# Memory rows leave the attention's sum after its column-tiled products, and TensorE's order is searched anew

## The chip, the cores and the metric

The kernel runs on one core of one Trainium2 chip. The metric is the device time of an execution in microseconds (us).

## The reference, cut to what matters

Two layers run one after the other, each an attention with recurrent memory and a gated FFN. The attention goes through 64 segments of 32 rows. Eight memory rows, the first rows of a segment's output, are put ahead of the next segment's rows:

```python
mem = mem0
for s in range(n_seg):                                   # 64 segments
    h = jnp.concatenate([mem, xs], axis=1)               # 8 + 32 rows of 576
    q, k, v = (jnp.einsum('btd,dhe->bhte', h, W) for W in (Wq, Wk, Wv))   # 32 heads of 128
    p = _softmax(jnp.where(mask, q @ k * scale, -1e9))
    o = jnp.einsum('bhte,hed->btd', p @ v, Wo)
    mem = o[:, :M, :].copy()                             # M = 8
    outs.append(o[:, M:, :])
```

So a segment's Q, K and V cannot be complete before the last output product of the segment ahead of it. (The three einsums and the score lines are shortened here.)

## The kernel before

The kernel runs both layers as a pipeline: in most of the 71 steps one segment of each layer is worked on, 2 x 40 columns side by side. TensorE runs its groups of matmuls in an order that is written down as a string of letters. The string was found by a search; a planning model in Python then fills in the other engines' order and the buffers.

The letters that matter: Q = a part of Q and K (32 products of 128x128 weights with 80 columns), q = its tail (rows 512 to 575 of the width 576, row-tiled), S = scores, T = transposes of the probabilities, P = probabilities times V, O = output product of a group of eight heads (32 products), o = its tail (output columns 512 to 575, column-tiled, 8 products), V/v and X/x = values, F/f = FFN up, W = FFN down (8 products), a, b, n, p = transposes for normalisations and residuals.

The sum of the output products is one PSUM bank, YB, with five chunks of columns: 0 to 3 from O, 4 from o.

```python
def wo(self, t, g, ot):                       # O
    ...
            for db in range(4):
                self.mm(yT[:, db, :], self.T.WO[:, GH * g + hl, db * P:(db + 1) * P], OT[:, hl, :], ...)

def wo_tail(self, t, g, ot):                  # o
    ...
            r = R64 * (hl % 2)
            self.mm(yT[r:r + R64, 4, :], self.T.WO[:, GH * g + hl, 4 * P:D], OT[:, hl, :], ..., tile_position=(0, r))
```

At the end of a step ScalarE copies the memory rows of chunks 0 to 3 from YB to HT, the transposed input rows of the next step. I call this "the copy". Chunk 4 comes in two halves that have to be added: ScalarE copies one to YO, VectorE adds the other. The dependencies that the planning model is given:

```python
yo = node("ACT", actc(c80), em.y_odd(t), deps=wots[3:], ...)
if nxt:
    ye.append(node("ACT", actc(4 * m), em.y_mem(t, nxt, 0), deps=wos[3:], prio=t - 0.01, name="Ymem"))
    ye.append(node("DVE", dve(m, m), em.y_mem(t, nxt, 1), deps=[yo] + ye, prio=t - 0.005, name="Ymem"))
ht_mem[t + 1] += ye
yts = [node("ACT", actc(*([128] * nl)), em.yts(t, ls, 0), deps=wos[3:] + ye, ...)]
```

`wos` are the step's O groups, `wots` its o groups. The copy depends on the last O alone, so the model may put it between the o groups. It is only a plan of the order: the semaphores come afterwards, from what the instructions of the program in that order read and write.

## Time and profile before

| | before |
|---|---|
| median time, 3 runs | 2802.13 us (2796.95 to 2804.0) |
| TensorE busy | 2730.5 us, 98% |
| VectorE, ScalarE busy | 72%, 40% |
| TensorE waits, YB products behind the copy | 43 of 70 steps |

TensorE has something in flight nearly always, so its busy share tells little of what could be saved. What does is the spacing of matmul starts: within a group it is steady, and between two groups it is nearly the same for the same pair of letters every time, unless something is waited for. From the records of start times I summed three things: spans from the first to the last start of each group (2279.2 us), usual pauses between groups (475.4 us), and excess over the usual pause (42.0 us, counting excesses above 0.06 us). All pauses together are 504.8 us, 12.6 less than the last two give, as many pauses are a little shorter than the usual one. The records follow the order string, except that 16 of the 60909 products (all in o groups) start up to 0.05 us ahead of the last product of a group of scores. The lines of the profile are shown in the prediction.

### The profile page before, as it was taken

Reading aid. Unit: us, or ns where it says so; the run is one execution under the profiler, and the core shown is the slowest. Engines: PE = TensorE matmul, PEld = TensorE weight load, DVE = VectorE, ACT = ScalarE, POOL = GpSimd, SP = SyncE. Lnnn points to the kernel's source line nnn. Section 1 sums busy time; section 2 is a strip of 40 time slices with the busy share of each in tenths; the row PEclk is TensorE's granted clock in tenths of the full one; section 3 lists DMA queues with packets and bytes.
Section 4 is the critical chain, followed back from the end, with each engine's and each line's share of the span. In section 5 each row is a group of like instructions: output and inputs, shape, how many; then the busy total and the mean of one; then the engine's idle time right before and its main releaser. Section 6 shows DMA issues by size and latency. Waiting matters only on the chain.

```text
span 2798.6 us, 136339 instructions
## 1 busy us (share of the span) xinstructions
PE 2730.5 (98%) x60909; PEld 2252.9 (81%) x60909; DVE 2018.1 (72%) x5501; ACT 1116.7 (40%) x3422; POOL 328.4 (12%) x399
## 2 busy tenths in 40 slices
PE   5999999999999999999999999999999999999998
PEld 4787878888888888888888888888888788888886
DVE  4677777777777677777767777776777777677765
ACT  2434443443434344343434434343443434343332
POOL 1111110110101011010101101010110101010110
PEclk9999999999999999999999999999999999999999
DMA  8072524234251523425152342515234251423568
GB/s 306 17 197 83 162 67 138 65 112 130 62 153 48 152 73 111 132 60 153 49 148 77 111 131 60 150 52 145 81 111 131 60 147 54 142 82 109 143 177 248
DMA packets 483438, 323.80 MB, mean 116 GB/s; under 512 B 26297, under 2 KB 478401, under 8 KB 481185
## 3 DMA queue, kind: packets, MB, share of 16 engines
q1 hardware_dynamic: 479824, 308.15, 37.6%
q8 instruction: 476, 7.80, 1.2%
q0 software_dynamic: 3024, 6.93, 0.8%
q14 instruction: 114, 0.93, 0.1%
HBM read 310.26 MB, written 2.36 MB: 112 GB/s over the span
## 4 chain that ended last, share of the span: by engine, by line
PE 96%; DMA 1%; ACT 1%; issue 1%; DVE 1%; POOL 0%; SPq 0%; DVEq 0%; ACTq 0%; POOLq 0%
PE bank L538 83%; PE YB L538 14%; DMA W<-in_A_Wk_dram 1%; ACT HT L541 0%; DMA W<-in_A_Wq_dram 0%; ACT OT L541 0%; DVE STAT L544 0%; DVE SME L544 0%; DVE PB L544 0%; ACT PTS L541 0%; DVE HTT L544 0%; ACT SME L541 0%; DVE PTS L544 0%; DVE XR L544 0%; DVE XN L544 0%
## 5 line engine op out<-in xcount | busy, mean ns | idle before, releaser
L538 PEld LDWEIGHTS <-W 128*128 128x128 bf16 (+1 forms) x29040 | 1227.2, 98 | 158.8 <-issue 53.6
L538 PE MATMUL bank<-HT,W 128*128 128x80 bf16 (+3 forms) x22720 | 815.5, 198 | 20.4 <-DMA W<-in_A_Wk_dram 11.7
L538 PE MATMUL bank<-XTB,W 128*128 128x256 bf16 (+3 forms) x6320 | 654.6, 262 | 1.4 <-issue 1.3
L895 POOL MEMSET PB<- 128x1024 bf16 x284 | 270.0, 951 | 2119.2 <-PE bank L538 1682.6
L541 ACT ACTIVATE QKT<-bank 128x64 bf16<-128x64 f32 (+1 forms) x1381 | 316.1, 315 | 364.2 <-PE bank L538 335.5
L538 PE MATMUL YB<-OT,WO 128*128 128x80 bf16 (+3 forms) x11360 | 429.4, 199 | 20.6 <-ACT HT L541 13.5
L538 PEld LDWEIGHTS <-WO 128*128 128x128 bf16 (+1 forms) x11400 | 389.0, 101 | 55.8 <-issue 39.3
L538 PE MATMUL bank<-WV,HT 128*32 128x512 bf16 (+1 forms) x6840 | 384.4, 382 | 0.0
L544 DVE CAST QKT<-bank 128x64 bf16<-128x64 f32 (+2 forms) x683 | 186.2, 316 | 238.7 <-PE bank L538 236.7
L541 ACT ACTIVATE HTT<-bank 128x512 bf16<-128x512 f32 (+1 forms) x324 | 177.8, 551 | 392.9 <-PE bank L538 391.5
L538 PE MATMUL bank<-W2C,HTT 128*128 128x288 bf16 x2232 | 320.7, 287 | 0.4 <-DMA W2C<-in_B_w_dram 0.4
L544 DVE TENSOR_REDUCE STAT<-SME 104x8 f32<-104x320 f32 (+1 forms) x568 | 271.8, 479 | 51.3 <-ACT SME L541 47.0
L544 DVE TENSOR_TENSOR PB<-SME,STAT 40x128 bf16<-40x128 f32 (+1 forms) x1004 | 283.5, 321 | 15.5
L538 PEld LDWEIGHTS <-HT 128*32 128x32 bf16 (+1 forms) x6840 | 149.4, 95 | 166.8 <-issue 42.8
L538 PEld LDWEIGHTS <-HTT 128*128 128x128 bf16 x2304 | 206.4, 98 | 59.2 <-issue 6.9
L544 DVE SCALAR_TENSOR_TENSOR XR<-bank,XR 128x288 f32<-128x288 f32 x576 | 239.6, 448 | 11.7 <-PE bank L538 7.2
L544 DVE SCALAR_TENSOR_TENSOR HTT<-HTT,bank 128x512 bf16<-128x512 bf16 (+1 forms) x324 | 201.9, 623 | 55.4 <-ACT HTT L541 53.4
L541 ACT ACTIVATE PTS<-bank 128x320 bf16<-128x320 f32 (+1 forms) x413 | 157.1, 414 | 177.6 <-PE bank L538 120.9
L544 DVE TENSOR_TENSOR HTT<-HTT,bank 128x512 bf16<-128x512 bf16 (+1 forms) x324 | 203.5, 628 | 22.3 <-PE bank L538 0.5
L541 ACT ACTIVATE OT<-bank 128x320 bf16<-128x320 f32 (+1 forms) x379 | 147.0, 412 | 171.1 <-PE bank L538 170.9
L541 ACT ACTIVATE SME<-SME 104x320 f32<-104x320 f32 (+1 forms) x284 | 133.5, 470 | 202.5 <-DVE SME L544 202.3
L544 DVE TENSOR_TENSOR SME<-bank,maskb 104x320 f32<-104x320 f32 (+1 forms) x284 | 133.9, 485 | 104.6 <-PE bank L538 102.8
(64 smaller groups left out, 1671.4 us busy)
## 6 DMA issues: line engine op xcount, KB each, us to landing
W<-in_B_w_dram SPq DMA_DIRECT2D x612, 256.0 KB, 3.8
W2C<-in_B_w_dram SPq DMA_DIRECT2D x306, 288.0 KB, 3.2
W<-in_B_w_dram SPq DMA_DIRECT2D x612, 32.0 KB, 3.4
W<-in_B_w_dram SPq DMA_DIRECT2D x10, 512.0 KB, 8.7
WO<-in_A_Wo_dram SPq DMA_DIRECT2D x4, 1152.0 KB, 18.3
XR<-in_A_x_dram POOLq DMA_DIRECT2D x16, 288.0 KB, 4.6
W<-in_A_Wq_dram SPq DMA_DIRECT2D x4, 1024.0 KB, 8.0
W<-in_A_Wk_dram SPq DMA_DIRECT2D x4, 1024.0 KB, 16.8
```

The source lines that it names most:

```text
L538: self.ch("PE", self.nc.tensor.matmul(out, lhsT=lhsT, rhs=rhs, start=start, stop=stop, skip_group_check=True, **k))
L541: self.ch("ACT", self.nc.scalar.activation(*a, **k))
L544: self.ch("DVE", getattr(self.nc.vector, fn_)(*a, **k))
L895: return lambda n: self.ch("POOL", self.nc.gpsimd.memset(self.T.PB[:, pb.i], 0.0))
```

## The change

The intent: the copy and the later row copies are ordered behind all column-tiled products of their step, and TensorE's order is searched again under that rule. The core of the diff:

```diff
-            ye.append(node("ACT", actc(4 * m), em.y_mem(t, nxt, 0), deps=wos[3:], prio=t - 0.01, name="Ymem"))
+            ye.append(node("ACT", actc(4 * m), em.y_mem(t, nxt, 0), deps=wos[3:] + wots, prio=t - 0.01, name="Ymem"))
...
-        yts = [node("ACT", actc(*([128] * nl)), em.yts(t, ls, 0), deps=wos[3:] + ye, prio=t + 0.01, rel=[y], name="YTS")]
+        yts = [node("ACT", actc(*([128] * nl)), em.yts(t, ls, 0), deps=wos[3:] + wots + ye, prio=t + 0.01, rel=[y], name="YTS")]
```

Of the three order strings only the one for four steps is shown, which runs 11 times. The other two (start and end) are replaced as well, and cut here:

```diff
 FOUR = (
-    "QQpqqQQqqVSSvnQQqqFTQqPfSVvQTFfqPOOSooTWFfPWFTOPfFOfooQQqqQQSqqVXxvWTQWFfqFQqPfSSWFWQfqXxFTWQqfPOTOooSWFfPFTOfPW"
-    "OooWFQfqQFfqWQFfqWQFfqVSSVvvQQqqWTWQPqSQTFfqFfPSWOWFTfoOPoTWPOOooabWQQqqpQQSqqQQqqVSSvXxTQqQqPTSXPxOToOPoTOPnOoo"
+    "QQqqQpQqqSVVvvQTQqPqSnQQSqqOFTFPffoSXxTOWWFPfoTFPfOOFooWQqfQFfqQWQSqqXVxvQTQqqWWFSSfPFQfqOFTQqfFPfoSWWOTFPfoTOFf"
+    "PWOooWQQqqFQqfSWQWQqqFQSfqVvTFWQqPfSWFQfqTOFfPoSWWFVvfTOPoTWPOOooabWQQqqQQSqqQQqqVSSvXxTQqPQqTOPSXxoTOPopTOPoOon"
 )
```

More of the change, by code (lines that the diff above doesn't have):

```diff
@@ L187 @@
 FIRST = (
-    "amQQqqQSqQqQSqQTQqqQSqSVvVvPXTPTOoOPoTOPoOoxQQqqQQSqqQSqVvQqQTSQPqqOTSoPTPOOToPaOooQQqqQQSqqQQSqVqvTQSqQPqVSTOPv"
-    "oTOoPXTOPOxooQQqqQSQqqQSqQqVSvQqTQqPTSOPToPOOTooPOoVvpQQqqQSQqqnVSvFfTQQqqQFPqfSFQfqXSTFfPOTOoWPxoTOFfPFOooWQqQq"
-    "fFfSQQqqWQSQqqVvTFfPSFTfPQOQFfqqOTSWFooPfFTOPoaOoWfQQqqFQfqSVvWQFfqQqVSvWQqFfTQqFPfSTQqOWFofSPTFfPOWTOoPObooQQqq"
-    "XxSQQqqQQqqSTQVqvQqSPSTXxOPoTOPToPOOooQQqqpQQqqSVvnQQqqSTFfPFQqfSOTQqPFWOFffSVoTvXPxWOTFofPFOofoQQqqQqSQWQqqVvTQ"
-    "PSFfqQFqfSXxWTQFqPfOToSFafPOFofOTWPFOfooQFqfWQqVvSQqQFfqFQfqSQTWqQqPSFQqfVSvTWOPFFffoTOPoTWPOoOboQQqqQQSqqXVvxSQ"
@@ L193 @@
-    "TpQqqXPxSQqTQqPOSoTOPoOTPnOooQQqqQpQSqQqqQnqVSvQTFfqFSPfVvQFfqTOFPfXxoSWWOTFfPXFTxofPOWOWooQQqqQqSQWFqfQQqqSTWFF"
-    "ffVvSQPqWTFQOqPfoSWTOFfPoFTOPfWOWooQFfqQqWFWQqfSVvFQqWfSFQqfQqWTQQPSqqVFTSvfPOWWoTFfOPoTWPOOooabQQqqpQQSqQqqVXxv"
-    "STQQqqQPqSTOSoPXxOTWPTnoPOOoo"
+    "maQQqQQqSqQqqSQqQQqqSSTVvVPTPvTOoPOToXOPxoOoQQqqQQSqqQqSQqVQqvSTQqPTSOPOToPoTOPoOoaQQqqVSvQQqqQQqqSTVSPvQqQqTOSP"
+    "oXTOPoTOPoOoxQQqqQQSqqQqSQVvqQSTqQqPSOoTPTOPoTOPoOoQQpqqQQqqSVSvQnQqqFTFffVSPvQTQqPqOFfOTFoSoPfWOXxTFfPFOoofWQQq"
@@ new lines @@
+    "qQQSqqFQfqSFWQfqVvSTQqPFTQfPqOSWoFTOPfoFTOfPWOooFQQqqfaQFfqSWQQqFfVvQSqqWTFFffVPvSWQQqqOSTFfPFfToOWoPTPOOoobQQqq"
+    "QQSqqXQxSqQTQqVvqSPQTqOPSXxToOPoTOPoOoQQpqqQQSqqVVSvvQnTQqqQPqSQTFfqFOfPSoTOFoPfXxOTFPfWOooFQfqFQqfQWQSqqVvSQWQq"
+    "qQTFqfSPQTFqfXxSFOofPWOTFfPoTaFfPOOWooFQqfQQqqFQqfVSvWQFqfQFSqWQSfqQTFfqVSvWPFfTFfPOToWPOoTOPobOoXxQpqQQqqXxSQQq"
+    "qVSTvQqPQqSTQqOPSoTOPoOTPonOoQQqqQpQqqSVVvvQTQqSqPQQSqqnOTFfPFoSfXxTFfPOWWFTOofPFOfooWFWQqfQQqqFQqfXxSWWQQqqVSvT"
+    "FQfqFQPfqSTOWWaFoSPfFTOofPWTOPFWOFooffVvWQQqqQqSQWFfqQQTqqSWFfPSQOTWqFfPFQqfVSoWWFTfvOPoTWPOOoobQQpqqVQSqvQQqQqS"
@@ L196 @@
+    "qQSqXTxQqPTSXxPOoTOPoTWPOOoon"
 )
 FOUR = (
-    "QQpqqQQqqVSSvnQQqqFTQqPfSVvQTFfqPOOSooTWFfPWFTOPfFOfooQQqqQQSqqVXxvWTQWFfqFQqPfSSWFWQfqXxFTWQqfPOTOooSWFfPFTOfPW"
-    "OooWFQfqQFfqWQFfqWQFfqVSSVvvQQqqWTWQPqSQTFfqFfPSWOWFTfoOPoTWPOOooabWQQqqpQQSqqQQqqVSSvXxTQqQqPTSXPxOToOPoTOPnOoo"
+    "QQqqQpQqqSVVvvQTQqPqSnQQSqqOFTFPffoSXxTOWWFPfoTFPfOOFooWQqfQFfqQWQSqqXVxvQTQqqWWFSSfPFQfqOFTQqfFPfoSWWOTFPfoTOFf"
+    "PWOooWQQqqFQqfSWQWQqqFQSfqVvTFWQqPfSWFQfqTOFfPoSWWFVvfTOPoTWPOOooabWQQqqQQSqqQQqqVSSvXxTQqPQqTOPSXxoTOPopTOPoOon"
@@ L200 @@
 )
 LAST = (
-    "QQqqVvpQQSqqQnQSqqQqTFPQfqVvSFOTFPfoSfTOPXxWFfOWTFofPFOooWWQfqQqFQfqSWQqXVvxSQWQqqFTfQFPfqSTOWWQPqFoSfFTOfPoWTOP"
-    "WOooFQqfQFfqQVSvqWQWFfqFSQfqQqWTWFSfPQQqqWFfSTWOFfPoVvTWPOoTOPobOoQQqqQQSqqQQpqqVSvSQqQTqXxSPTXxPOToOPoTWPOOoonQ"
-    "QqqpQqSVvQnQqqQSqTFfPVSvQQqqFTOPoSfOTFWWofPFTOfPXOWooQxqWQFqfVvSQQqFfqQQSqqQqTFfPSWWFQfqFfOWWFTSofPFTOWPfoTFPfOO"
-    "WooQQqqFQQqfqSWFWQFqffSVvWTWQQqqQqVSSvFPfFTOWWfFPfToOPoTWOPoOWboQQqqpQqSVXnvxQFfqQQqqTSSQPqFfQFfqWTSOPFTOofPFTof"
-    "POOooWQFqfQFfqQQSqqVSvWQQqqTQPqSFQqfVTFfPvSOTOXooxPWTFPOOfooQQqqQFSqfVQFqfvWQTFSqQfqQFqPSfQqWTOPoSFfTOoPFWTOfPFO"
@@ L207 @@
-    "fooQQqqQQSqqVvQWQSqqVvSQTQqPqTOPSoTFPOoOTofPOopnWFfFFfFffWFWfFfFfFfWFfWFfFFffWFfWFfFFffWFfFfWW"
+    "QQpqqQQSqqVvnQFfqQSqQTqFPfFTOSPQqfVOWvoSoTFPWOTfXxoPFOfoWFWQqfQQqqFQSqfXVxvWWQTFqfSFQqfQqQqPSFTWOWPfSoTOPFWOToof"
+    "PFOfoWQQqqVvFQfqSWWFQfqFQqfQqSWTFPfQQSqqWTFSPfVvWTWOFfoOPoTWPOoOobQQqqQpQSqqQQqqSXVxSvQqTQPqTXxPSOOoTWPToPOOoonQ"
+    "QpqqVSvQqQQnqqQTFPSqfQQSqqOFTfVvPFToSfPOWOooWTFPfXOWxoWQQqqVSvFQqfQqFQQqqfSTFPfQSqWWOFTQqfFPfoSTWWFOPfoTFPfWWOOF"
+    "oofFQqQfqQqSWQWFqfFfTQQSqqQWqWFQqfSVvFfPSWOWTFfPVovTWPTOoPOOoobWQQQqqqpQSVXqxvQSnQqqFfTQSPqQFqfOFToSfPWTOFPfoTOP"
@@ L208 @@
+    "FOfooWQQqqQFqfSQFqfVSvQQqqQTWFqfPSQTqFOoSfPVvFTOPWTOoofPFOoXfxQWQqqVSvQFfqQFqfQSqWTQFfqQSqQPqFTSOfPoWTOPFTofPOOo"
+    "oFQqQqfQQSqqWQSqVvQTQQqqqSPSTVPvFOOTooPfTOoPOopnWFFffFfFWfFfFWfFfFfWFfFfWFfFWfFfFWfFFffWFfFfWW"
 )
```

## The prediction

> **What bounds the kernel now.** I read the page first, then the list of waits, then the timeline around the places that the list named. The page, the kernel before:
>
> ```profile
> span 2798.6 us, 136339 instructions
> ...
> PE 2730.5 (98%) x60909; PEld 2252.9 (81%) x60909; DVE 2018.1 (72%) x5501; ACT 1116.7 (40%) x3422; POOL 328.4 (12%) x399
> ...
> PEclk9999999999999999999999999999999999999999
> ...
> PE 96%; DMA 1%; ACT 1%; issue 1%; DVE 1%; POOL 0%; SPq 0%; DVEq 0%; ACTq 0%; POOLq 0%
> ```
>
> TensorE is busy in all 40 slices at full clock and carries 96% of the chain that ended last. The time is therefore the sum of three terms: the matmuls themselves, the pauses between unlike groups of them, and TensorE's waits. The change leaves the first alone, so I have to size the other two.
>
> The list of waits (engine and tile waiting, the releaser, then total us, times, longest us):
>
> ```profile
> ACT HT L541 <- PE YB L538: 120.4, 70, 3.0
> ...
> PE bank L538 <- DVE XN L544: 13.8, 3, 10.2
> ...
> PE YB L538 <- ACT HT L541: 13.5, 43, 0.3
> ...
> PE bank L538 <- DMA W<-in_A_Wk_dram: 11.7, 5, 4.4
> ...
> PE bank L538 <- ACT HT L541: 2.9, 6, 1.5
> ...
> PE YB L538 <- ACT OT L541: 1.8, 6, 0.4
> ```
>
> HT holds the transposed input rows, and the 70 ScalarE writes to HT from YB are the memory rows (8 per layer) leaving the sum YB for the next step; there are 71 steps. The third line is the surprise: in 43 of the 70, TensorE, which is still adding products into YB, waits for that copy. The lines about XN and Wk belong to the start, where inputs are loaded. The timeline shows one of the 43:
>
> ```profile
> 1369.32 0.93 PE L538 MATMUL YB<-OT,WO 128*128 128x80 bf16 x22
> ...
> 1370.29 0.22 ACT L541 ACTIVATE HT<-YB 128x64 bf16<-128x64 f32 x1 [1.01 <-PE YB L538]
> 1370.57 0.33 PE L538 MATMUL YB<-OT,WO 128*64 128x80 bf16 x8 [0.32 <-ACT HT L541]
> ...
> 1370.84 1.86 PE L538 MATMUL bank<-HT,W 128*128 128x80 bf16 x47
> 1370.94 0.23 ACT L541 ACTIVATE YO<-YB 64x80 f32<-64x80 f32 x1 [0.42 <-PE YB L538]
> ```
>
> The 128*128 products are output chunks 0 to 3 of a group of eight heads, the 128*64 ones the column-tiled half chunk 4. In TensorE's order this place reads "OooQQ": last group, two column-tiled groups, next step's Q and K. The copy lies between the two column-tiled groups: it waited for the first (which is within the top line, merged), and the second waited for it. The copy ended at 1370.51, the second group began 0.05 us later. From the start times of the matmul records, the pause between two such groups (last matmul's start to next first one's) is 0.033 us where nothing waits and 0.519 us here. Without the wait the step's Q could have begun 0.486 us earlier, if its rows were there.
>
> **What the Trainium skill says.** "PSUM — Partial Sum Buffer", section "PSUM bank collisions raise a hardware error": two engines must not touch the same bank and quadrant at once, even at disjoint columns, so software guards by bank. The trace agrees: the copy reads chunks 0 to 3 and the waiting products write chunk 4, different columns, and still they wait for each other. "TensorEngine Tiling (Array Packing)", "Key Properties": changing the tiling mode drains TensorE. The trace agrees: a pause within the full mode after an 80-column product is 0.036 us, from full to row or column tiles 0.132 to 0.134, back 0.131 to 0.134; leaving the 32-column value products costs 0.309 and their tails 0.318. "TensorE: Matmul & The Clock Gate", "Architectural detail": matmuls stay in program order. So the order string decides what can stand in front of a waiting product, and the 43 waits hold up everything behind them.
>
> **The change, part by part.** The two dependency lists sit in the planning model. They do not add a semaphore by themselves; they decide where the copy and the later row copies stand against the column-tiled products. The model before let the memory copy start 0.22 us after group O, in between the column-tiled groups; now it comes after the last of them. No instruction is added or removed: counted by letter, the old and the new order have the same 3931 groups.
>
> *Removed.* 43 waits of 0.519 - 0.033: the sum over the records is 20.8 us. At other boundaries before, Q waited for the copy directly (five places, 1.7 us in excess of the usual pause); these are replaced as well.
>
> *Added.* The copy now starts after the last column-tiled group. A place of the old order already looks like this ("OoQQ"):
>
> ```profile
> 2487.48 0.22 ACT L541 ACTIVATE HT<-YB 128x64 bf16<-128x64 f32 x1 [0.65 <-PE YB L538]
> 2487.73 0.23 ACT L541 ACTIVATE YO<-YB 64x80 f32<-64x80 f32 x1
> 2487.75 1.92 PE L538 MATMUL bank<-HT,W 128*128 128x80 bf16 x49 [0.34 <-ACT HT L541]
> 2487.76 1.81 PEld L538 LDWEIGHTS <-W 128*128 128x128 bf16 x49 [0.32 <-issue]
> 2487.99 0.37 DVE L544 TENSOR_TENSOR HT<-YB,YO 64x16 bf16<-64x16 f32 x2 [2.11 <-ACT YO L541]
> ```
>
> From the last column-tiled matmul's start to the copy I find 0.244 us where ScalarE is free, the copy takes 0.223, and TensorE goes on 0.052 later: 0.519 us in which TensorE needs other work. Directly followed by Q it has 0.134 of pause, so it would lose 0.385. I went through the 70 boundaries of the new order. In the four-step block, which runs 11 times, three of four have a W group (second FFN product) ahead of Q: 0.134 + 0.867 + 0.123 = 1.124 us, more than 0.519, so no loss. The fourth has "OonQQ": five transposes give 0.424, so 0.095 is lost, 11 times, 1.0 us. The first and last steps, by the same count, lose 2.1 us (four bare "oQ" make 1.4 of it). Sum added: 3.2 us. The half chunk's memory rows come later, over YO and VectorE: in the place shown they end 1.15 us after the last column-tiled matmul; the earliest row-tiled Q/K product that needs them comes 2.37 us after it in the new order. No loss.
>
> *Moved.* The order has 2152 mode changes against 2150. Giving each neighbouring pair the median pause of its first letter and the mode it goes to, as measured before (waits taken out), the pauses sum to 475.4 us for the old order and 472.9 for the new: -2.5 us.
>
> *Other waits.* All pauses beyond those medians sum to 42.0 us before: 20.8 as above, 1.7 of Q, 5.2 in two start and end places (the first Q, and the last normalisation behind the last attention rows), 14 scattered. To see if the scattered ones grow, I took the shortest distances that the records bear (0.62 us between the probabilities' transposes and the product with V, 0.66 from there to the output product, 4.3 us for a softmax, and four more) and summed what each order falls short of: 14.1 us before, 15.0 after. I carry +1.
>
> The sum: 2802.1 - 20.8 - 1.7 + 3.2 - 2.5 + 1 = 2781.3 us, 0.7% less.
>
> **The rivals.**
> *The wait only moves.* Memory rows leave later, so each Q might wait in place of the column-tiled product. With nothing in between, 70 times 0.385 = 27 us would be added: 2802 - 22.5 + 27 - 2 = 2805. Against it: the W groups at three of four boundaries; but they come from elsewhere, where they covered a wait too. The shortfall sum says that little is uncovered, without modelling how ScalarE and VectorE queue.
> *The search gained more than the rule.* A new order may also shorten the scattered 14 us. Were all of it gone, and the pauses lower by 5 more, the time would be near 2762. The distances speak against much of that: value products to their use got closer (10th percentile 3.4 us, before 5.9), transposes to the V product wider.
> *Another engine's order upsets it.* VectorE is 72% busy, ScalarE's queue is served in order, and a copy that waits longer for the column-tiled groups holds back evictions behind it. ScalarE already idles 120.4 us ahead of these copies; an added 0.3 us a step is 21 us of idle time in an engine 40% busy. Where an eviction behind it is urgent, TensorE would wait: perhaps a third of the steps, +7 us, 2788.
>
> **Range and chances.** The terms that I can count leave 2781. The scattered waits may go 10 us either way, and the three runs before spread over 7 us. Range 2770 to 2793. Faster by over 2% needs 56 us, more than all waits of TensorE that I found (42 us); slower by over 2% would need them to more than double. Chances 0.01, 0.98 and 0.01.
>
> **What would show it.** Right: the list of waits has no "PE YB" behind "ACT HT", "PE bank" behind "ACT HT" stays under some 6 us, and the timeline of a middle step shows the copy after all 128*64 products with a W2C group over it. TensorE's matmul groups keep their busy times. Wrong: "PE bank" behind "ACT HT" near 15 to 25 us (the first rival); or waits behind QKT, PTS, OT or V copies grown by more than 10 us (the third); or pauses that fall although no wait did (the second).

## The result, and the profile after

| | before | after |
|---|---|---|
| median of 4 runs | 2801.5 us | 2782.38 us |
| lowest to highest | 2796.95 to 2804.0 | 2779.84 to 2784.87 |

The ratio is 0.9934, with a 95% interval of 0.9916 to 0.9951. (Ratios are the mean time of one kernel's runs over that of the other's of the same rounds, so not quite the ratio of the medians.) The page of the kernel after:

```profile
span 2782.7 us, 136378 instructions
...
PE 2725.4 (98%) x60909; PEld 2245.9 (81%) x60909; DVE 2041.0 (73%) x5559; ACT 1093.0 (39%) x3364; POOL 328.4 (12%) x399
...
PE 96%; DMA 1%; DVE 1%; issue 1%; ACT 1%; POOL 0%; SPq 0%; DVEq 0%; ACTq 0%; POOLq 0%
```

The same number of matmuls, the same bound. The shares say nothing of the 16 us that the span lost. The list of waits of the kernel after does:

```profile
ACT HT L541 <- PE YB L538: 150.4, 65, 5.7
...
PE bank L538 <- DMA W<-in_A_Wk_dram: 12.6, 4, 4.6
...
PE bank L538 <- DVE XN L544: 8.5, 2, 5.1
...
PE bank L538 <- ACT HT L541: 5.1, 8, 1.7
...
PE YB L538 <- ACT OT L541: 3.9, 15, 0.4
```

"PE YB" behind "ACT HT" (13.5 us, 43 times before) is gone from the list. "PE bank" behind "ACT HT" (Q behind ScalarE's writes of HT, the copy among them) rose from 2.9 to only 5.1 us. ScalarE waits longer for the sum (150.4 us, before 120.4), without a wait of TensorE to match. The new plan also gives VectorE 58 instructions that were ScalarE's (5501 to 5559, and 3422 to 3364). The timeline of a middle step's end, where the order reads "OooWQQ":

```profile
638.42 0.61 PE L538 MATMUL YB<-OT,WO 128*128 128x80 bf16 x17
...
638.96 1.15 PE L538 MATMUL bank<-W2C,HTT 128*128 128x288 bf16 x8
639.10 0.22 ACT L541 ACTIVATE HT<-YB 128x64 bf16<-128x64 f32 x1 [2.04 <-PE YB L538]
...
639.95 0.74 PE L538 MATMUL bank<-HT,W 128*128 128x80 bf16 x16
```

The first line holds the last O product and both o groups (1 + 8 + 8 products). The copy comes after them and lies wholly under W; when W ends, Q's rows have been there for 0.6 us, and no wait stands ahead of Q. The end of the fourth step of the block, "OonQQ", has the five transposes in W's place:

```profile
713.28 1.57 PE L538 MATMUL YB<-OT,WO 128*128 128x80 bf16 x40 [0.26 <-ACT OT L541]
...
714.79 0.45 PE L538 MATMUL bank<-ident,XN 128*128 128x128 bf16 x5
714.90 0.22 ACT L541 ACTIVATE HT<-YB 128x64 bf16<-128x64 f32 x1 [1.66 <-PE YB L538]
...
715.17 0.63 PE L538 MATMUL bank<-HT,W 128*128 128x80 bf16 x13
```

The copy ends at 715.12 and Q starts 0.05 us later: here the transposes are about 0.1 us too short. This is below what the profile marks as idle, so no bracket shows it; the starts do. The first line of this fence shows the other wait that is left in each block: O waits for the eviction of OT (0.26 us in the bracket, 0.33 by the starts).

By the sums of starts, before to after:

| TensorE | before | after |
|---|---|---|
| first matmul at | 10.2 us | 4.8 us |
| inside groups | 2279.2 | 2282.6 |
| between groups, all | 504.8 | 490.8 |
| of it: usual pauses, by the table of before | 475.4 | 472.9 |
| of it: excess over them | 42.0 | 29.4 |
| of the excess: second o behind the copy | 20.8 (43) | 0 |
| Q behind the copy, o or n ahead of it | 1.7 (5) | 3.0 (17) |

The first matmul comes 5.4 us earlier because the tiny transposes of the initial memory now stand ahead of those that need the normalised input; the next group then waits 5.2 us for that input. The two cancel. The 3.4 us more inside the groups lie in the first 60 and the last 231 groups (2.1 and 1.6 us), where some groups wait for weights that are still being loaded; the 3640 groups between take 2119.5 and 2119.2 us. Part of it is scatter, as the same kernel, profiled again, had 2285 us in all groups. But the three profiles with the old order strings and seven buffers have 2278 to 2280 us and the five with the new ones 2280 to 2285, so that the new start and end cost a little is not ruled out.

### The profile page after: what moved, and what is told of

Read it like the earlier page. It is cut to its first block, busy times and chain, and to the rows that moved or that the text cites. A ratio compares the mean times of both kernels' runs of the same rounds, so it can differ in the third digit from the quotient of the medians.

```text
span 2782.7 us, 136378 instructions
## 1 busy us (share of the span) xinstructions
PE 2725.4 (98%) x60909; PEld 2245.9 (81%) x60909; DVE 2041.0 (73%) x5559; ACT 1093.0 (39%) x3364; POOL 328.4 (12%) x399
## 4 chain that ended last, share of the span: by engine, by line
PE 96%; DMA 1%; DVE 1%; issue 1%; ACT 1%; POOL 0%; SPq 0%; DVEq 0%; ACTq 0%; POOLq 0%
PE bank L538 83%; PE YB L538 13%; DMA W<-in_A_Wk_dram 1%; DMA WO<-in_B_w_dram 0%; DVE STAT L544 0%; ACT OT L541 0%; DVE PB L544 0%; DMA W<-in_A_Wq_dram 0%; DVE SME L544 0%; ACT HT L541 0%; ACT SME L541 0%; DVE XR L544 0%; ACT PTS L541 0%; DVE PTS L544 0%; ACT QKT L541 0%
## 5 line engine op out<-in xcount | busy, mean ns | idle before, releaser
L544 DVE CAST QKT<-bank 128x256 bf16<-128x256 f32 (+2 forms) x682 | 184.1, 317 | 186.9 <-PE bank L538 185.5
L538 PE MATMUL bank<-W2C,HTT 128*128 128x288 bf16 x2232 | 312.9, 287 | 0.0
L541 ACT ACTIVATE OT<-bank 128x320 bf16<-128x320 f32 (+1 forms) x352 | 138.1, 413 | 214.7 <-PE bank L538 214.6
L541 ACT ACTIVATE V<-bank 128x512 bf16<-128x512 f32 x248 | 138.4, 596 | 181.6 <-PE bank L538 181.2
```

Source lines behind the costliest of these rows:

```text
L538: self.ch("PE", self.nc.tensor.matmul(out, lhsT=lhsT, rhs=rhs, start=start, stop=stop, skip_group_check=True, **k))
L541: self.ch("ACT", self.nc.scalar.activation(*a, **k))
L544: self.ch("DVE", getattr(self.nc.vector, fn_)(*a, **k))
```

## The experiments

Each run is a change of one thing. In each batch the kernel before ran in the same rounds, at 2802.2 us in the first and 2802.8 us in the second (the runs with the copy issued twice and with six buffers, and the half chunk in its own bank).

### The rule with the old order

The two new dependency lists in the kernel before, and its order strings:

```diff
-  ... em.y_mem(t, nxt, 0), deps=wos[3:], ...
+  ... em.y_mem(t, nxt, 0), deps=wos[3:] + wots, ...
-  ... deps=wos[3:] + ye, ...
+  ... deps=wos[3:] + wots + ye, ...
```

> The old order strings with the two new dependency lists. Theory (the gain needs both parts: the rule takes the copy out from between the column-tiled products, and other work between those and the next Q hides it): the 43 waits of TensorE's YB products for the copy (20.8 us) are gone, but in the old order 32 boundaries go straight from the last column-tiled group to Q, so Q waits instead: by my count 15.3 us in place of 22.5, and 2 to 3 us more where the copy now stands behind a tanh on ScalarE. 2795 to 2799 us, ratio to before 0.998 to 0.999; in the list of waits PE bank behind ACT HT rises from 2.9 to 12 to 18 us and PE YB behind ACT HT is gone. Rival A (the rule alone is the gain): 2780 to 2784. Rival B (the rule does nothing, the search is the gain): 2800 to 2803 with the YB waits still there.

Measured: 2793.0 us (ratio 0.9967, 0.9952 to 0.9982). It is 2 us under the range that I gave, within what runs differ by. The mechanism is the one expected. From the list of waits:

```profile
PE bank L538 <- ACT HT L541: 15.4, 40, 1.5
```

and from the timeline, at the place that the prediction showed ("OooQQ"):

```profile
1369.05 0.22 ACT L541 ACTIVATE HT<-YB 128x64 bf16<-128x64 f32 x1 [1.18 <-PE YB L538]
1369.30 0.23 ACT L541 ACTIVATE YO<-YB 64x80 f32<-64x80 f32 x1
1369.33 0.84 PE L538 MATMUL bank<-HT,W 128*128 128x80 bf16 x19 [0.34 <-ACT HT L541]
```

The wait has moved from the second o to Q. By the starts, 39 places with 16.4 us in all, against 20.8 + 1.7 before: the rule alone is worth 6 us of waits (by the times 9 us, where the interval gives 5 to 13). It is worth something since the second o now runs ahead of the copy and no longer between it and Q: at this place Q starts 0.95 us after the last O product's start, in the kernel before 1.05.

### The new order with the old rule

```diff
-  ... em.y_mem(t, nxt, 0), deps=wos[3:] + wots, ...
+  ... em.y_mem(t, nxt, 0), deps=wos[3:], ...
-  ... deps=wos[3:] + wots + ye, ...
+  ... deps=wos[3:] + ye, ...
```

> The new order strings with the two old dependency lists. Theory: the plan puts the copy ahead of the last column-tiled group at 45 of 70 boundaries, at 30 of them with just one group left, so some 25 to 30 waits of 0.486 us come back: 12 to 14.5 us on top of the new kernel's 2782, so 2793 to 2798 us; PE YB behind ACT HT near 8 to 10 us in 25 to 30 places. Rival A (the rule is the gain): 2800. Rival B (the searched order is the gain, whatever the rule): 2780 to 2784.

Measured: 2794.19 us (0.9974, 0.9957 to 0.9991). The list of waits:

```profile
PE YB L538 <- ACT HT L541: 8.5, 27, 0.3
```

27 waits are back, 13.0 us by the starts. So the new order does not help by itself at those places: a W that stands behind the o group cannot cover a wait of the o group. With the order alone there are 16 fewer than before.

Together with the run below, the four cells are 2802.2 (neither), 2793.0 (rule), 2794.2 (order) and 2782.5 (both): -9, -8 and -20 us. Neither rival with one cause holds. That the two parts need each other shows in the waits: those at the copy, by the starts, are 22.5, 16.4, 15.9 and 3.0 us, so the two alone remove 6.1 and 6.6 us and together 19.5. The times do not show it by themselves: 9 and 8 add to 17 of the 20 us, and each of them is known to about 4 us.

Only the first of the two lists matters. With the second list alone put back in the new kernel, the instruction streams of four engines are unchanged, and on ScalarE two neighbouring copies change places, once, at the end. I did not run that; it is read from the plans.

### The new kernel again

> The new kernel unchanged, as the yardstick on this chip: 2780 to 2785 us, ratio to before 0.992 to 0.995.

Measured: 2782.52 us (0.9932, 0.9917 to 0.9947).

### W taken away from over the copy

In the new kernel, two of the four boundaries of the block; the groups and the sum of the pauses stay:

```diff
-"...OFooWQqfQFfq..."        -"...WOooWQQqqF..."
+"...OFooQWqfQFfq..."        +"...WOooQWQqqF..."
```

> The new kernel, with the first Q and the W ahead of it exchanged at two of the four boundaries of the repeated block (22 of 70 boundaries), so that Q follows the last column-tiled group directly. Pauses between groups sum to the same. Theory (W covers the copy): 22 waits of 0.385 us, 8.5 us: 2789 to 2793 us; PE bank behind ACT HT rises from 5.1 by 6 to 9 us. Rival (the copy is not on TensorE's path, whatever stands there, as Q's rows are only needed later): 2780 to 2785 and no new waits.

Measured: 2792.24 us, 9.7 us more than the new kernel in the same rounds (0.9966 against 0.9932). Its list of waits has

```profile
PE bank L538 <- ACT HT L541: 12.7, 30, 1.7
```

that is 22 waits more than the new kernel's 8, as many as exchanges. The place where the kernel after had W over the copy:

```profile
637.75 0.22 ACT L541 ACTIVATE HT<-YB 128x64 bf16<-128x64 f32 x1 [2.04 <-PE YB L538]
638.00 0.23 ACT L541 ACTIVATE YO<-YB 64x80 f32<-64x80 f32 x1
638.02 0.77 PE L538 MATMUL bank<-HT,W 128*128 128x80 bf16 x17 [0.34 <-ACT HT L541]
```

Q starts 0.544 us after the last o product's start, where it would take 0.134 without a wait: 0.41 us lost, 22 times, 9.0 us. At the third boundary with a W, Q could not be put directly behind the o group: there it also needs rows that the transposes a and b bring, and the planning model could not go on.

### The copy issued twice, in both kernels

```diff
+                    for _ in range(2):
-                    self.cp(n, o..., pick(yT[:, 0:4]))
+                        self.cp(n, o..., pick(yT[:, 0:4]))
```

> The kernel before, with the copy of the memory rows issued twice in a row (same data, same result). Theory (the copy's own time lies on TensorE's path wherever a column-tiled group or Q stands behind it: 43 + 5 places): 48 times 0.20 to 0.24 us, 9.5 to 11.5 us: 2810 to 2815 us; PE YB behind ACT HT rises from 13.5 to 22 to 24 us. Rival (the copy is hidden and the 43 waits are bookkeeping): 2800 to 2804.

Measured: 2815.49 us, 12.7 us more than before and half a us over my range. The 43 waits grew from 20.8 to 31.7 us, 0.25 us each, and in 12 places where the copy had just been out of the way of an o group it no longer is (3.8 us). I had left these 12 out. Together that is 14.7 us in the profiled execution; the 2 us to the 12.7 are within what executions differ by. Its list of waits:

```profile
PE YB L538 <- ACT HT L541: 27.9, 57, 0.6
```

> The new kernel with the copy issued twice. Theory (the copy is on the path only where too little stands between the last column-tiled group and Q: 13 places with the five transposes, 4 with nothing, 3 where Q waits for later ScalarE work): 20 times 0.22, 4.4 us: 2785 to 2790 us. Rival (the copy is on the path of every step): 70 times 0.22, 15 us: 2796 to 2800.

Measured: 2791.0 us, and 1 us over my range. The new kernel did not run in this batch; against its 2782.4 us of before it is 8.6 us more, by the two ratios to the kernel before (0.9959 and 0.9932) 7.6, where I had expected 4.4. The pauses of the profiled execution grew by 7.7 us. By the starts: the 13 places with transposes 3.3 us, the 4 with nothing 1.0, the three with b ahead of Q 0.7. What I had missed is 11 waits of 0.17 us (1.9 us) at "OooabWQQ". The list of waits has them behind VectorE ("PEld" are TensorE's weight loads, which wait with the products), and the timeline shows one:

```profile
PEld L538 <- DVE HT L544: 3.5, 11, 0.3
```

```profile
687.96 0.48 ACT L541 ACTIVATE HT<-YB 128x64 bf16<-128x64 f32 x2 [2.05 <-PE YB L538]
...
688.42 1.14 PE L538 MATMUL bank<-W2C,HTT 128*128 128x288 bf16 x8
688.46 0.23 ACT L541 ACTIVATE YO<-YB 64x80 f32<-64x80 f32 x1
...
688.73 0.35 DVE L544 TENSOR_TENSOR HT<-YB,YO 64x16 bf16<-64x16 f32 x2
689.11 0.54 DVE L544 COPY HT<-bank 128x240 bf16<-128x240 bf16 x3
...
689.55 0.72 PEld L538 LDWEIGHTS <-W 128*128 128x128 bf16 x19 [0.30 <-DVE HT L544]
```

The copy itself ends at 688.44, long before W does. But the copy to YO stands behind it in ScalarE's order, VectorE's additions of the half chunk wait for YO, and behind these VectorE copies the rows that the transposes b brought, which Q reads too: of the three merged copies the second ends at 689.495, and Q starts 0.057 us later. In the kernel after, that copy ends 0.13 to 0.14 us before Q, so W has just some 0.08 us of slack at one of the three covered boundaries. Still, a doubled copy costs far less in the new kernel than 70 times 0.22 (15 us), and less than in the old one.

### The half chunk in a bank of its own

All eight banks are in use, so a yardstick is needed first: the kernel before with six buffers in the pool.

```diff
-POOLS = {"bank": 7, "y": 1, ...
+POOLS = {"bank": 6, "y": 1, ...
```

> The kernel before with six PSUM buffers in the pool in place of seven: the yardstick for the next run, which needs the eighth bank. 2805 to 2860 us; the 43 waits of PE YB behind ACT HT stay (12 to 14 us).

Measured: 2838.36 us (1.0126), with "PE YB" behind "ACT HT" at 13.5 us and 43 times as before. Then chunk 4 in the freed bank; old order, old dependency lists:

```diff
+    T.YH = pp.tile([P, 512], F32, name="YH")
...
-                self.mm(yT[r:r + R64, 4, :], ..., False, ...)
+                self.mm(self.yh(t)[r:r + R64, :], ..., g == 0 and hl < 2, ...)
```

(and in the three places that read it).

> As the run with six buffers (old order, old dependency lists), with the half chunk of the attention's sum in a bank of its own, so that the copy and the column-tiled products share no bank. Theory (the sharing of a bank is what makes TensorE wait): no wait of PE YB behind ACT HT, and Q hardly waits as the copy starts right after the last full product: 19 to 24 us less than with six buffers. Rival (the wait only moves to Q): at most 5 us less, and PE bank behind ACT HT up by over 10 us.

Measured: 2816.53 us, 21.8 us less than with six buffers. No wait of "PE YB" or "PE YH" behind "ACT HT" is left. The boundary "OooQQ" again:

```profile
1379.47 0.48 PE L538 MATMUL YH<-OT,WO 128*64 128x80 bf16 x16
1379.57 0.22 ACT L541 ACTIVATE HT<-YB 128x64 bf16<-128x64 f32 x1 [0.74 <-PE YB L538]
...
1379.88 0.89 PE L538 MATMUL bank<-HT,W 128*128 128x80 bf16 x20
```

The copy runs beside the 16 column-tiled products, and Q follows without a wait. So the 43 waits come from sharing the bank, and from nothing in the data. YH is a tile of its own as well as a bank of its own; whether the semaphores were set because of the one or the other, this run does not tell. It is no way to a faster kernel: the bank costs 36 us elsewhere.

No run beats the new kernel. What is left of waits above 0.06 us in a block of four steps is 0.33 us ahead of O and 0.09 to 0.12 us ahead of Q. The W at "abWQQ" cannot be spared for them: it has almost no slack, as the doubled copy showed.

## Why the prediction was right

Predicted 2781 us, measured 2782.4. That it fits to 1 us is partly luck, as executions differ by up to 7. Between the two profiled executions, the pauses with the first start are 19.4 us less (14.0 and 5.4), where the prediction's terms sum to 20.8; the 3.4 us more inside the groups were not foreseen. Its terms, one by one:

- *Removed, 20.8 us in 43 waits:* they are gone, and the run with the half chunk in its own bank shows that the shared bank (or tile) caused them: 21.8 us without touching order or rule.
- *Added, 3.2 us:* by the starts 3.0 us in 17 places, 13 with transposes (1.45 us) and 4 with nothing (1.6 us). The covered boundaries showed no wait. That W is what covers them is shown by the exchange (+9.7 us for 22 boundaries, estimated as 8.5). The size for a bare Q was a little low: 0.385 predicted, 0.41 measured.
- *Moved, -2.5 us of pauses:* these come from a table of before's pauses, and the part that neither table nor waits explain changed by 1.1 us. Too small to be shown by the times. The prediction read 0.309 and 0.318 us as what it costs to leave the 32-column products. Most of that is not the change of mode: within these modes the pause is already 0.203 to 0.206. It used the whole pauses, so its sum stands.
- *Other waits, +1 us:* without the start and the end they went from 14.3 to 15.6 us. That the sum stayed is partly luck: 12 waits of an O that follows n (3.6 us) went, and of an O that follows o there are 16 (4.8 us) where there were 3 (0.8 us). The shortest distances that it counted with were not the shortest on record: in steps with one layer there are 0.47 us (it used 0.62) and 0.55 (0.66).
- *The first rival* (the wait only moves) is what the rule alone does: 16.4 of 22.5 us came back at Q. With the new order it did not happen.
- *The second rival* (the search gained more than the rule) falls: the new order under the old rule gains 8 us, no more than the rule alone, and the scattered waits did not shrink.
- *The third rival* (ScalarE's queue in order) did not cost the 7 us that I gave it in the new kernel. But the doubled copy shows that a chain through ScalarE's and VectorE's orders is near at one boundary in four.

One thing was left out: I took three W boundaries as equally safe, by W's length against the copy's chain. At "OooabWQQ" the slack is some 0.08 us, since a second chain, over YO and VectorE, runs behind the copy. It happened to fit.

## What to carry to other kernels

In this kernel a read of a part of an accumulator made the products that were still to come wait, though they write other columns of the same bank (0.519 us in place of 0.033, 43 times). It helped to place the read behind the last product, and to put work that needs none of it between that product and the first reader of the copied rows. Count from the trace what is needed: last product's start to the copy, the copy, and the way back. Here it was 0.52 to 0.54 us, and either half of the cure alone gave less than half of the gain. Count also what stands behind the read in its engine's order, as the 0.08 us at one boundary show.

## What the Trainium skill lacked or had wrong

- "PSUM — Partial Sum Buffer", "PSUM bank collisions raise a hardware error": it gives the rule to guard by bank, but not what the guard costs. Here a ScalarE read of 64 columns between two groups of matmuls took the pause between their starts from 0.033 to 0.519 us; 43 of them made 20.8 us, and 21.8 us went when the columns got separate banks.
- "TensorEngine Tiling (Array Packing)", "Key Properties": mode changes drain TensorE, without a figure. Here, from the last start to the next first start: 0.036 us within the full mode (80 columns), 0.128 to 0.134 between full, row and 64-column tiles, 0.309 to 0.318 out of the 32-column tiles with 512 columns, where 0.203 to 0.206 is usual within their modes. Compared with the pause of the same group within its mode, a change adds 0.09 to 0.12 us nearly everywhere; the 2150 changes add some 211 of the 475 us of pauses.
- "TensorE: Matmul & The Clock Gate", "Back-to-back issue gap": it states about 81 ns per matmul for 128 columns and 131 ns for 512 in a real stream of weight loads and matmuls, and says that its formula for an isolated matmul (columns by 2.4 GHz, and 2.5 ns) under-counts there at small sizes and over-counts at large ones. In this kernel the stream follows that formula: 35.8 ns for 80 columns (1.111 us over 31 starts), 56.5 ns for 128 (groups of 16, median of 72), 109 ns for 256 and 124 ns for 288 (0.867 us over 7; the formula gives 122.5), with a weight load for each matmul.
